# Hash attention and a gated block: three reorderings in how weight pieces are prepared

## The chip, the cores and the metric

The kernel runs on one core of one Trainium2 chip. The metric is device microseconds of that core for one whole execution; three runs of the kernel before are given, and one profiled execution with its trace.

## The reference

Attention: q, k and v are (4, 8, 768, 64). Each row of q and k is hashed with `proj` to six sign bits; a score counts only where both have the same six bits.

```python
mask = q_bucket[:, :, :, None] == k_bucket[:, :, None, :]
scores = np.where(mask, scale * np.matmul(q, k.transpose(0, 1, 3, 2)), -1e9)
attn = softmax(scores)
x = (attn @ v).transpose(0, 2, 1, 3).reshape(3072, 512)
g = x @ w_gate
out = (g / (1 + np.exp(-g)) * (x @ w_val)) @ w_out     # w_gate, w_val: 512 x 1536; w_out: 1536 x 512
```

All of it is to have fp32 accuracy.

## The kernel before

**Precision by parts.** The gated block multiplies in a faster 32-bit format and makes up for it by splitting each operand into a high part, a low part and a difference. A product is then two groups of matmuls: an `a` group (high and low, 16 matmuls) and an `n` group (differences, 8 matmuls), combined by a copy of `a` with a scale and a subtraction of `n`. All matmuls of the block are recorded on L713.

**Pieces.** The three weight matrices come as 64-bit words. They are cut into 36 pieces of 128 x 512 numbers, in the order in which they are used. `scale` (L139, L140, ScalarE) takes a piece's words apart; `widths` (L153, L155, L158, VectorE, three steps) puts the bits into fp32; `round_up` (L146, ScalarE) makes the high part; `parts` (L166, L168, VectorE, two steps) makes the other two and stores all three in DRAM (L170). `widths` ends with the load of a later piece's words (L130), three pieces on. A piece's buffer of words is one of three, its stage one of two pairs. `bring` (L251) fetches a stored piece into a ring of six buffers, on the POOL queue; in the gated block the other transfers go by SP's queue.

**Attention.** It works through 16 pairs of heads (iterations n = 0 to 15). Each scores 12 units, exponentiates them on ScalarE, adds them up on VectorE for the row sums, and multiplies by v. The row sums of pair n are made in iteration n + 1: `total` (matmuls, L590), a row copied by ScalarE (L595), a small transfer `few<-row` (L597), then `invert`: a reciprocal on VectorE (L603), a transfer to DRAM (L605) and two that spread it over partitions (L612, tile `r`). `norm` (L619) multiplies the attention output by `r` and stores it (L623). `settle()` runs the inversions that are waiting. In iteration 15 it runs twice, once at the start (pair 13) and once after the scores (pair 14); pair 15 is inverted and normalized inside the gated block, after its 6th and 14th atom. In each iteration some pieces are scaled, widened and kept (stored): 24 are scaled by the end, 22 kept.

**The gated block.** The 3072 tokens go in three blocks of 1024. Within a block there are 12 up products (U0 to U11, one per 128 columns of the hidden layer) and four down products (D0 to D3, each over three of the U); the order is U0 to U3, D0, U4 to U6, D1, U7 to U9, D2, U10, U11, D3. A U has four atoms: gate `a` with its copy (L752), gate `n` with its correction (L758) and silu (L760), value `a` with its copy (L752), value `n` with its correction (L758), the product with the gate (L762) and the hidden high part (L763). The two other hidden parts (L769, L772, the "tail") are written out after the next atom. A D has eight atoms, one per 128 tokens, here called chunks o0 to o7: nine matmuls, then in D0 a copy (L813, ScalarE) and a subtraction (L819, VectorE), in later D a multiply-add (L815) and a subtraction, both on VectorE. (D3 has four atoms more.)

**PSUM.** All products of the block take turns in four two-bank buffers, in order of creation. The `a` and the `n` of one U thus use buffers 0 to 3, and a chunk of D one buffer.

**What sets the order.** The schedule is written out by hand: every engine carries out its instructions in the order in which the code issues them. Between the atoms the block deals out preparing steps from `turns()`. One turn is, for the piece that was widened in the turn before (the old one) and the next (the new one): a rounding, a scaling, two `parts` steps, three `widths` steps; seven steps. The first turn has two old pieces and nine steps. How many steps follow each atom is a tuple: (1, 2, 2, 2) in a U, and (1, 2, 2, 1, 1, ...) in a D.

Of the kernel before, what the change touches and what calls it, by code (L numbers as in the profile page):

```python
# [19 lines left out]
def kernel(  # L20
# [68 lines left out]
    def finish(todo):  # L89
        while todo:  # L90
            todo.pop(0)()
# [31 lines left out]
    def load_words(count, queue=None):  # L123
        queue = queue or queues[0]
        for i in range(len(words), min(count, NPIECE)):
            words[i] = t = wordp.tile([P, PIECE, 2], I32, tag="words", name="words")
            to = t.rearrange("p f w -> p (f w)")
            if len(pieces[i].shape) == 3:
                to = to.rearrange("p (j c) -> p j c", j=NJ)
            queue.dma_start(to, pieces[i])  # L130

    def scale(i):
        t = words[i]
        if i // 2 not in stages:
            stages[i // 2] = stagep.tile([P, 2, 3, PIECE], FP32, tag="stage", name="stage")
        staged[i] = st = stages[i // 2][:, i % 2]
        top = t.rearrange("p f w -> p (f w)").bitcast(U16)
        top = top.rearrange("p (f w) -> p f w", w=4)[:, :, 1]
        nc.scalar.activation(st[:, 1], t[:, :, 1].bitcast(FP32), AF.Copy, scale=2.0**-112)  # L139
        nc.scalar.activation(t[:, :, 0], top, AF.Copy, scale=2.0**-13 * (1 + 2.0**-17))  # L140
        progress["scaled"] = i + 1

    def round_up(i):
        if i not in rounded:
            st = staged[i]
            nc.scalar.activation(r32(st[:, 0]), st[:, 1], AF.Copy, scale=TOWARD)  # L146
            rounded.add(i)

    def widths(i):
        t, st = words[i], staged[i]  # L150
        lo, hi = t[:, :, 0], t[:, :, 1]
        wi = st[:, 1].bitcast(I32)
        nc.vector.tensor_single_scalar(wi, wi, 3, op=ALU.logical_shift_left)  # L153
        yield True
        nc.vector.scalar_tensor_tensor(out=wi, in0=hi, scalar=-(1 << 31), in1=wi,  # L155
                                       op0=ALU.bitwise_and, op1=ALU.bitwise_or)
        yield True
        nc.vector.tensor_tensor(wi, wi, lo, op=ALU.add)  # L158
        added.add(i)
        load_words(i + 4)  # L160
        yield True

    def parts(i):
        st = staged[i]
        w = st[:, 1]
        nc.vector.tensor_tensor(r32(w), w, st[:, 0], op=ALU.subtract)  # L166
        yield True
        nc.vector.scalar_tensor_tensor(out=r32(st[:, 2]), in0=w, scalar=-STEP,  # L168
                                       in1=st[:, 0], op0=ALU.mult, op1=ALU.add)
        queues[0].dma_start(ram[i].bitcast(FP32), st)  # L170
        progress["kept"] = i + 1
        yield True

    def begin_pieces(count):
        for i in sorted(added - rounded):
            round_up(i)
        for i in range(progress["scaled"], min(progress["scaled"] + count, NPIECE)):
            load_words(i + 1)
            scale(i)

    def keep_pieces():
        for i in range(progress["kept"], progress["scaled"]):
            if i in added:
                for _ in parts(i):
                    pass

    def widen_pieces():
        for i in range(progress["kept"], progress["scaled"]):
            if i not in added:
                for _ in widths(i):  # L190
                    pass

    def turn():

        old = [i for i in sorted(added) if i >= progress["kept"]]
        new = progress["scaled"]

        def first():
            for i in old:
                round_up(i)  # L200

        def second():
            if new < NPIECE:
                load_words(new + 1)
                scale(new)

        yield first
        yield second
        for i in old:
            steps = parts(i)  # L210
            for _ in range(2):
                yield lambda: next(steps)
        if new < NPIECE:
            more = widths(new)
            for _ in range(3):
                yield lambda: next(more)
# [88 lines left out]
    def attention(scope):  # L305
# [39 lines left out]
        def load(n, names):  # L345
            if n < len(pairs):
                for name in names:
                    fetch(n, name, nc.sync)
# [187 lines left out]
        def score(u):  # L536
            if u % (2 * NCH):
                products(u)
                mark(u)
            else:  # L540
                banks_of[u] = two_banks("sc")[:, :, 0:HQ]
                product(u, bits, True, False)
                product(u, T, False, True)
                mark(u, False)
# [84 lines left out]
        def prepare_pair(count):  # L629
            for _ in range(count):  # L630
                if steps:
                    rest.extend(f for f in steps.pop(0)() or [] if f)

        def settle():
            while waiting:
                last.append(waiting.pop(0)())
# [11 lines left out]
        for n in range(len(pairs)):  # L648
            u = 2 * NCH * n
            more = n + 1 < len(pairs)  # L650
            if n == 1:
                widen_pieces()
            if n and more:
                steps = front(n + 1)
                prepare_pair(2)
            widen_pieces()
            settle()
            for i in range(2 * NCH):
                if u + i > 2:
                    score(u + i)  # L660
                if n == 0 and i == TURN:
                    prepare_pair(2)
                if i % NCH and i < 2 * NCH - 1:
                    add(u + i)
                if i == (2 if n else TURN):
                    load(n + 2, "qk")
            row = total(n - 1) if n else None
            if more:
                prepare_pair(1)
            finish(rest)  # L670
            add(u + 2 * NCH - 1)
            if row:
                row()
            finish(last)
            if not more:
                settle()
            begin_pieces(PACE[n])
            finish(splits)
            splits.extend(later)
            later.clear()  # L680
            for c in range(2 * NCH):
                attend(u + c)
            load(n + 2, "v")
            keep_pieces()
            if n >= len(pairs) - 3:
                bring()
# [14 lines left out]
    def gated_block(scope):  # L701
# [184 lines left out]
        def split_x(block, pr):  # L886
            return split(raw_x.pop((block, pr)), block, pr, 0, WB)
# [3 lines left out]
        for kind, n in order:  # L891
            b, f = divmod(n, NF if kind == "U" else NF // NQ)
            changing = b + 1 < NB
            if changing:
                if (kind, f) == ("D", NF // NQ - 2):
                    load_x(b + 1, range(NP // 2))
                elif kind == "U" and f >= NF - 2:
                    assert len(added) == NPIECE
                    splits.extend(split_x(b + 1, f - NF + 2))
                    if f == NF - 1:  # L900
                        load_x(b + 1, range(NP // 2, NP))
            if n == NB * NF // NQ - 1 and kind == "D":
                finish(tails)
            for at, atom in enumerate(atoms_of(kind, n)):
                tail = atom()
                finish(tails)
                if tail:
                    tails.append(tail)
                if changing and kind == "U" and f >= NF - 2 and at:
                    splits.pop(0)()  # L910
                if changing and kind == "D" and f == NF // NQ - 1:
                    if at == 0:
                        more = [split_x(b + 1, pr) for pr in range(NP // 2, NP)]
                        for x in more:
                            x.pop(0)()
                    if at in (7, 10):
                        for x in more:
                            x.pop(0)()
                count[0] += 1
                if left and count[0] in (6, 14):  # L920
                    left.append(left.pop(0)())
                    left[:] = [f for f in left if f]
                for _ in range(((1, 2, 2, 2) if kind == "U" else (1, 2, 2) + (1,) * 9)[at]):
                    step = next(mine, None)
                    if step:
                        step()
# [35 lines left out]
```

## Time and profile before

| What | Value |
|---|---|
| median of 3 runs | 911.25 us (910.28 to 911.82) |
| the profiled execution | 910.49 us, span in the trace 908.7 us |
| granted TensorE clock | 0.999 |
| attention, until the first matmul of the gated block | 314.80 us |
| D1, 72 matmuls | 16.32 us |
| VectorE busy, 300 to 400 us | 76.69 us |
| ScalarE busy, 300 to 400 us | 52.20 us |
| DMA, mean over the span | 192 GB/s |

A row of the page or of a timeline has a start, a duration, the engine, the line of the code and the operation, what is written and read (out<-in) with shapes, a count, and in brackets how long the engine had been idle before and what ended the idle time. PE is TensorE's matmul, PEld its weight load, DVE VectorE, ACT ScalarE, POOL GpSimd and SP SyncE (SPq: its queue). The chain of waits is followed back from the last instruction to what released each step.

### The profile page before, as it was taken

The numbers are of one execution on the slowest core, as the hardware profiler recorded it, in microseconds if no ns is written. First come the engines' busy times: TensorE is split into PE (matmuls) and PEld (weight loads), VectorE is DVE, ScalarE is ACT, GpSimd is POOL, SyncE is SP. The second block draws the span as 40 slices with busy tenths as digits, with TensorE's granted clock in tenths as the row PEclk, the third lists the DMA queues.
The fourth block names the chain that finished last, engine by engine and source line by source line (L and its number), as shares of the span: only waits on it lengthen the run. The fifth ranks groups of instructions, "written<-read, shape, count | busy, mean of one in ns | idle before, by whom it ended". The sixth has DMA issues, their size and how long they took to land.

```text
span 908.7 us, 12452 instructions
## 1 busy us (share of the span) xinstructions
PE 902.4 (99%) x4801; PEld 636.5 (70%) x4801; DVE 664.9 (73%) x783; ACT 451.5 (50%) x606; POOL 88.6 (10%) x177
## 2 busy tenths in 40 slices
PE   9999999999999999999999999999999999999998
PEld 4444444444444588788888888888888888888886
DVE  6779999998988868779786856464658754474746
ACT  7788988788887655452514233331313243413220
POOL 1001100010001210001100000101000100001000
PEclk9999999999999999999999999999999999999999
DMA  7557888878877699776756563534434642525332
GB/s 183 107 144 182 191 209 188 206 205 224 232 196 208 217 393 335 262 268 241 270 189 239 207 244 105 178 136 168 145 139 162 237 151 95 201 70 209 104 139 93
DMA packets 143706, 174.24 MB, mean 192 GB/s; under 512 B 103360, under 2 KB 113568, under 8 KB 143648
## 3 DMA queue, kind: packets, MB, share of 16 engines
q0 software_dynamic: 22240, 114.83, 35.6%
q1 hardware_dynamic: 120000, 57.43, 24.7%
q10 hardware_dynamic: 1408, 1.20, 0.5%
q8 instruction: 38, 0.62, 0.3%
q14 instruction: 20, 0.16, 0.1%
HBM read 133.17 MB, written 39.42 MB: 190 GB/s over the span
## 4 chain that ended last, share of the span: by engine, by line
PE 58%; DVE 2%; ACT 1%; issue 1%; DMA 1%; DVEq 0%; ACTq 0%; SPq 0%
PE a L713 26%; PE o L713 20%; PE n L713 13%; DMA words<-in_moe_w_out_dram 1%; DVE hid L769 0%; DVE g L758 0%; ACT v L752 0%; DVE stage L155 0%; DVE v L762 0%; DVE v L758 0%; ACT hid L763 0%; DVE o L819 0%; DVE stage L158 0%; DVE hid L772 0%; ACT o L813 0%
## 5 line engine op out<-in xcount | busy, mean ns | idle before, releaser
L713 PE MATMUL a<-xparts,ring 128*128 128x512 f32 x1152 | 273.0, 389 | 0.0
L713 PEld LDWEIGHTS a<-xparts,ring 128*128 128x128 f32 x1152 | 216.1, 188 | 45.5 <-issue 0.6
L713 PE MATMUL o<-ring,hid 128*128 128x512 f32 (+1 forms) x870 | 198.8, 388 | 1.1 <-DVE o L819 1.0
L713 PEld LDWEIGHTS o<-ring,hid 128*128 128x128 f32 x870 | 162.7, 188 | 35.6 <-DVE o L819 2.0
L533 ACT ACTIVATE A<-sc 128x768 f32<-128x768 f32 x192 | 153.9, 816 | 0.9
L523 PE MATMUL sc<-qT,kT 64*128 64x384 f32 x768 | 152.8, 483 | 0.3 <-ACT qb L436 0.2
L713 PE MATMUL n<-xparts,ring 128*128 128x512 f32 x576 | 142.3, 389 | 0.0
L554 PE MATMUL av<-A,vraw 128*64 128x386 f32 (+1 forms) x768 | 127.7, 488 | 0.0
L713 PEld LDWEIGHTS n<-xparts,ring 128*128 128x128 f32 x576 | 108.1, 188 | 22.5
L758 DVE TENSOR_TENSOR v<-v,n 128x1024 f32<-128x1024 f32 x36 | 44.0, 1222 | 99.5 <-PE n L713 97.6
L251 POOL DMA_DIRECT2D ring<-ram x108 | 57.1, 531 | 497.9 <-PE n L713 315.4
L554 PEld LDWEIGHTS av<-A,vraw 128*64 128x64 f32 x768 | 53.7, 136 | 73.3 <-issue 63.0
L752 ACT ACTIVATE g<-a 128x1024 f32<-128x1024 f32 x36 | 36.9, 1026 | 127.7 <-PE a L713 126.9
L523 PEld LDWEIGHTS sc<-qT,kT 64*128 64x128 f32 x768 | 68.3, 187 | 41.3 <-issue 35.5
L763 ACT ACTIVATE hid<-v 128x1024 fp32r<-128x1024 f32 x36 | 38.2, 1062 | 109.0 <-DVE v L762 106.4
L760 ACT ACTIVATE g<-g 128x1024 f32<-128x1024 f32 x36 | 38.2, 1062 | 88.8 <-DVE g L758 88.8
L819 DVE TENSOR_TENSOR o<-o 128x512 f32<-128x512 f32 x92 | 63.0, 686 | 19.2 <-ACT o L813 16.9
L758 DVE TENSOR_TENSOR g<-g,n 128x1024 f32<-128x1024 f32 x36 | 43.8, 1216 | 34.9 <-PE n L713 34.9
L523 PE MATMUL sc<-qb,kb 64*128 64x384 bf16 x384 | 62.8, 323 | 0.0
L572 DVE SCALAR_TENSOR_TENSOR both<-A 128x1536 f32<-128x1536 f32 x32 | 55.4, 1732 | 6.0 <-ACT A L533 4.6
L769 DVE SCALAR_TENSOR_TENSOR hid<-hid,v 128x1024 fp32r<-128x1024 f32 (+1 forms) x39 | 44.5, 1141 | 19.7 <-ACT hid L763 19.7
L576 DVE TENSOR_TENSOR both<-both,A 128x1536 f32<-128x1536 f32 x32 | 55.9, 1748 | 1.7
(80 smaller groups left out, 692.6 us busy)
## 6 DMA issues: line engine op xcount, KB each, us to landing
ring<-ram POOLq DMA_DIRECT2D x108, 768.0 KB, 5.0
ram<-stage POOLq DMA_DIRECT2D x22, 768.0 KB, 4.3
ram<-stage SPq DMA_DIRECT2D x14, 768.0 KB
vraw<-in_v_dram SPq DMA_DIRECT2D x16, 384.0 KB
out_dram<-o SPq DMA_DIRECT2D x23, 256.0 KB
kraw<-in_k_dram SPq DMA_DIRECT2D x60, 96.0 KB
qraw<-in_q_dram SPq DMA_DIRECT2D x60, 96.0 KB
r<-sums SPq DMA_DIRECT2D x30, 192.0 KB
```

What stands on the lines that cost most here:

```text
L251: nc.gpsimd.dma_start(t.bitcast(FP32), ram[at].bitcast(FP32))
L523: nc.tensor.matmul(banks_of[u][:, h], x["k", n][rows, ks], x["q", n][rows, qs], start=start, stop=stop)
L533: nc.scalar.activation(weights(u)[:, :, 0:HQ], banks_of.pop(u), AF.Exp, scale=SCALE * (1.0 if units[u][0] else OFF / 2))
L554: nc.tensor.matmul(ps[h * D : (h + 1) * D, 0:width], raws["v", n][:, h, c, :], a[:, h, 0:width], start=c == 0, stop=c == NCH - 1)
L572: nc.vector.scalar_tensor_tensor(out=t, in0=first, scalar=S * EPS / P / 2, in1=now, op0=ALU.add, op1=ALU.add)
L576: nc.vector.tensor_tensor(t, t, now, op=ALU.add)
L713: nc.tensor.matmul(ps, w, x, start=start, stop=stop)
L758: nc.vector.tensor_tensor(two(z), two(z), n_, op=ALU.subtract)
L760: nc.scalar.activation(z, z, AF.Silu)
L763: nc.scalar.activation(h, val, AF.Copy, scale=TOWARD / STEP)
L769: nc.vector.scalar_tensor_tensor(out=l_, in0=h_.bitcast(FP32), scalar=-STEP, in1=v_, op0=ALU.mult, op1=ALU.add)
L819: nc.vector.tensor_tensor(accs[c], accs[c], t[:, 1], op=ALU.subtract)
```

## The change

Three edits. In a turn, the scaling of the new piece is issued in front of the rounding of the old one. In the last iteration of attention, `settle()` is called ahead of `widen_pieces()` (in the other iterations the order stays). In down products the numbers of steps after the atoms become 0, 1, 1, 1, ... so that a D of eight atoms has seven steps, where it had ten.

```diff
@@ turn()
+        yield second
         yield first
-        yield second
         for i in old:
@@ attention
             if n and more:
                 steps = front(n + 1)
                 prepare_pair(2)
-            widen_pieces()
-            settle()
+            if more:
+                widen_pieces()
+                settle()
+            else:
+                settle()
+                widen_pieces()
@@ gated_block
-                for _ in range(((1, 2, 2, 2) if kind == "U" else (1, 2, 2) + (1,) * 9)[at]):
+                for _ in range(((1, 2, 2, 2) if kind == "U" else (0,) + (1,) * 11)[at]):
                     step = next(mine, None)
```

`first` rounds the old pieces (L146), `second` loads the new piece's words if they were not loaded and scales it (L139, L140).

## The prediction

> **What bounds the kernel now.** I read the page's busy shares first. TensorE (PE) is busy 902.4 of 908.7 us, so only what stops PE counts.
>
> ```profile
> PE 902.4 (99%) x4801; PEld 636.5 (70%) x4801; DVE 664.9 (73%) x783; ACT 451.5 (50%) x606; POOL 88.6 (10%) x177
> ```
>
> Then the waits of PE over the whole run: after the start only one real stop, in the first down product (D0, products F = 0 to 3 being U0 to U3 before it). PE's timeline places it.
>
> ```profile
> 329.48 1.98 PE L713 MATMUL n<-xparts,ring 128*128 128x512 f32 x8
> ...
> 358.50 10.36 PE L713 MATMUL o<-ring,hid 128*128 128x512 f32 x45
> 369.86 5.49 PE L713 MATMUL o<-ring,hid 128*128 128x512 f32 x21 [1.00 <-DVE o L819]
> ```
>
> Products overlap by 0.2 us in this view, so U1's gate n ends at 329.48 + 1.98 = 331.46. D0's 72 matmuls take 16.32 us where nothing stops them (D1 in the chain of waits), and D0 begins when U3's last product ends, 356.68 + 1.98 = 358.66. It would end at 374.98; in the chain U4 begins at 376.70. So D0 loses **1.7 us**. That, and about 4 us of tail that the change doesn't touch, is all there is to win.
>
> Why does D0 stop? The timelines of ScalarE (ACT) and VectorE (DVE) through U1 show a ring of waits, one round per up product:
>
> ```profile
> 336.30 1.21 DVE L758 TENSOR_TENSOR g<-g,n 128x1024 f32<-128x1024 f32 x1
> ...
> 339.16 0.69 DVE L166 TENSOR_TENSOR stage<-stage 128x512 fp32r<-128x512 f32 x1 [0.96 <-ACT stage L146]
> 340.07 1.22 DVE L758 TENSOR_TENSOR v<-v,n 128x1024 f32<-128x1024 f32 x1 [0.22 <-ACT v L752]
> 341.33 1.23 DVE L762 TENSOR_TENSOR v<-g,v 128x1024 f32<-128x1024 f32 x1
> ...
> 344.94 1.22 DVE L772 TENSOR_TENSOR hid<-hid 128x1024 fp32r<-128x1024 f32 x1
> 346.08 0.68 DVE L155 SCALAR_TENSOR_TENSOR stage<-words,stage 128x512 int32<-128x512 int32 x1
> 346.69 1.21 DVE L758 TENSOR_TENSOR g<-g,n 128x1024 f32<-128x1024 f32 x1
> ```
>
> ```profile
> 337.55 1.06 ACT L760 ACTIVATE g<-g 128x1024 f32<-128x1024 f32 x1 [3.37 <-DVE g L758]
> 338.51 0.61 ACT L146 ACTIVATE stage<-stage 128x512 fp32r<-128x512 f32 x1
> 339.03 1.01 ACT L752 ACTIVATE v<-a 128x1024 f32<-128x1024 f32 x1
> 339.94 0.65 ACT L139 ACTIVATE stage<-words 128x512 f32<-128x512 f32 x1
> 340.49 0.66 ACT L140 ACTIVATE words<-words 128x512 int32<-128x512 uint16 x1
> 342.59 1.06 ACT L763 ACTIVATE hid<-v 128x1024 fp32r<-128x1024 f32 x1 [1.44 <-DVE v L762]
> ```
>
> By differences of starts: gate correction L758 to silu L760 1.25; to rounding L146 0.96; to v's copy L752 0.52; to v's correction L758 1.04; to L762 1.26; to L763 1.26; to L769 1.09; to L772 1.26; to L155 1.14; to the next gate correction 0.61. Sum **10.39 us**, and PE's round is 2 x (3.63 + 1.81) = 10.88. So the lag of a gate correction behind its n product falls by 0.49 a round: U1 336.30 - 331.46 = 4.84, U3 357.07 - 353.22 = 3.85. The lag comes from one late row before U0's correction, the normalizing L619 of pair 14, which waits for its reciprocals:
>
> ```profile
> 324.32 1.02 DVE L619 SCALAR_TENSOR_TENSOR xT<-xT,e,r 128x768 f32<-128x768 f32 x1 [5.88 <-DMA r<-sums]
> ```
>
> D0 meets what is left of it: output chunk 5 (o5) needs the PSUM buffer of o1, whose L819 lies behind L769, L772 and L155.
>
> **The Trainium skill.** "Perfetto Trace Analysis", section Identifying the Most-Contended Engine, warns that matmul busy is no measure of PE's roofline. The trace agrees: each matmul reads 389 ns but they come every 16.32/72 = 227 ns, so I count stops, not busy time. The same page, section Optimization Strategy, says that repeated gaps can mean too few PSUM buffers; here all products share four two-bank buffers, and D0's stops are waits for one. "ScalarE: Activation LUTs", section What ACT_TABLE_LOAD costs, gives 186 ns + 0.833 ns an element and 93 ns of overlap: an estimate of 612 ns for 512, against 610 for L146, and 612 - 93 = 519 in line, against 0.52 seen. I use the trace's. "DMA: Bandwidth & Descriptors", section Issuing engines are not separate DMA queues, says transfers of all queues share 16 engines. DMA share is 0.98 to 1.08 from 315 to 320 us, when r of pair 14 travels; so its landing can't be priced from its size.
>
> **Part 1, the reciprocals of the last pair ahead of widening.** In iteration 15, L603 of pair 13 runs at 300.25 after two widenings (3.8 us) and would run at 296.5. Its few-row was issued at 291.21 with DMA idle from 291, so it is there. r then lands 3.8 earlier and the 1.1 us wait ahead of its L619 (310.90) goes. All on DVE after it comes 1.1 earlier: L603 of pair 14 at 310.7, not 311.84. SP's queue: L605 and L612 of pair 13 leave earlier, so few<-row of pair 14 leaves right behind its ACT copy (306.8, not 308.07); its landing took at most 3.8 us, so by 310.7 it is there. The two L170 stores and the loads on POOL, queued behind the same DVE work, move 1.1 earlier too and still compete with r. Value taken: r of pair 14 lands at **323.2**. Bounds: 324.3 (no gain) and 319 (uncontended, as with pair 13, L612 to L619 about 4 us). PE in attention doesn't wait for any of this: 0.
>
> **Part 2, scaling (L139, L140) ahead of rounding (L146).** A turn is 7 steps and a U takes 7, so U1 to U3 repeat: step L155 | L158, then first-of-turn | second-of-turn, L166 | L168, L153. Before, the rounding sat ahead of v's copy and L166 came just after it. Now the pair of scalings sits ahead of the copy and the rounding behind it, and L166, which stands on DVE **ahead of v's correction**, waits for that rounding. The piece of the round from silu to v's correction becomes: L760 to L139 0.97, to L140 0.55, to L752 0.56, to L146 0.92, to L166 0.65, to L758 0.61 = 4.26, where it was 0.96 + 0.52 + 1.04 = 2.52. The round grows by 1.74 to **12.13 us**, above PE's 10.88: the lag now grows by 1.25 a round. Queued behind the waiting L166 are v's correction, L762, L769 and L772; PE waits for their buffers. The DMA side: the load call in the scaling finds its words loaded, and stores follow L168; neither queue is reordered within a turn. U0 rounds two pieces; its round is 11.04 before and, with both roundings behind silu, 11.40 after.
>
> **Part 3, D takes 7 steps, not 10 (0,1,1,1,... for 1,2,2,1,...).** L155 no longer lies ahead of o1's L819 (0.6 us saved) and L146 no longer blocks o2's copy for L158 (the 0.5 us second stop). But 7 steps a D keep the turn in the same phase, so U4 to U9 all have the 12.13 round, where 10 steps used to shift it. The preparing ends in D2, not U9. Counted in code order, piece 34 is stored in U9 and brought at D2's end, 35 stored two chunks before D2's end and brought after U10's gate: no bring is late at 4 to 9 us a landing. Steps in D2 lie on DVE beside 2.04 us a chunk: 0.
>
> **The sum.** L619 323.2, U0's correction 324.14, U1's 335.54, U2's 347.67, U3's 359.80 (lag 6.6). D0's chunks start every 2.04 from 358.66.
> - o1 needs U3's g n: 359.80 + 1.26 = 361.06, wanted 360.70: stop 0.35.
> - o2 needs v's copy: 359.80 + 1.25 + 0.97 + 0.55 + 0.56 + 1.04 = 364.17, wanted 363.1: 1.05.
> - o3 needs v's correction: about 366.55, wanted 366.2: 0.35.
> - o4 needs L819 of o0: v's correction 365.3, L762 366.55, L763 367.8, L813 368.8, L819 369.4, free 0.74 later 370.1, wanted 368.6: 1.5.
> - o5 needs L819 of o1 behind L769 and L772: 369.4 + 0.6 + 1.26 + 1.14 + 0.74 = 373.1, wanted 372.2: 0.95.
>
> D0: 4.2 us. D1: U4 starts without lag, U5 1.5, U6 2.8. From U6's correction to o1's free buffer in D1 (L758 to L762 6.77, L168 and L153 1.74, L815 and L819 of o0 1.67, L769 and L772 2.40, L815 and L819 of o1 1.46) is 14.04; + 2.8 = 16.8 against 5.44 + 5 x 2.04 = 15.64: 1.2 us. D2 repeats it: 1.2. After 6.6; before, the same working gives 1.4 of the 1.7 measured. Change **+5.2 us**. The profiled execution took 910.49 (span 908.7 and 1.8 around it): 915.7. The median of the runs is 0.76 above it: **916.4**.
>
> **Rivals.**
> - r of pair 14 lands by 320, uncontended: U0's correction is then bound by PE, U3's lag is 3.75; only o4 (0.5) and o5 (0.95) stop, with D1 and D2 3.9 in all, against 1.4: +2.5, 913.7. For it: pair 13's r took 4 us. Against: DMA is full from 315 on.
> - r doesn't move: lag 7.8 at U3, 1.1 us more: 917.5.
> - Not slower: DVE's wait for the rounding stays hidden, that is the round stays under 10.88. The place is L166 in U1 to U9; the price of being wrong is 1.25 us a round. If ACT's rounding does come before v's copy, the round is about 10.4, all stops go (-1.7) and the median is 909.6. Against: each engine starts its instructions in the order written in every row I read.
>
> **Chances.** Forecast 0.54, early r 0.16, unmoved r 0.16, hidden rounding 0.10, else 0.04. 0.2% (1.8 us) is what a measurement can tell; since only 1.7 can be won, hidden rounding is "same". Faster 0.03, same 0.11, slower 0.86. The range takes in both bounds of r: 913.0 to 918.4.
>
> **What would show it.** Right: in U1 to U3, L146 after L752 of v, DVE idle ahead of L166 for ACT L146, gate corrections 12.1 us apart, stops in D0 from o1 on and one of about 1.2 in D1 and in D2, L619 near 323.2. Wrong: gate corrections 10.9 or less apart, D1 without a stop, or a stop for a ring buffer.

## The result and the profile after

The changed kernel takes 916.0 us (median of 6 runs, 915.29 to 916.3) against 910.92 for the kernel before (6 runs, 910.26 to 911.82): a ratio of 1.0056, 95% interval 1.0045 to 1.0067, so 5.1 us slower. The profiled execution took 915.62, its span is 913.8. In the changed kernel the lines behind the second edit lie four further down: L752 is now L756, L758 is L762, L762 is L766, L763 is L767, L769 and L772 are L773 and L776, L813 to L819 are L817 to L823, the matmuls are L717. Kernels without the second edit keep the old numbers.

The busy shares of the page can't tell the two kernels apart.

```profile
PE 903.6 (99%) x4801; PEld 635.7 (70%) x4801; DVE 663.5 (73%) x783; ACT 450.8 (49%) x606; POOL 88.4 (10%) x177
```

PE's timeline can. The columns are start, duration, engine, line, operation; a bracket is idle time and what ended it.

```profile
358.09 2.20 PE L717 MATMUL o<-ring,hid 128*128 128x512 f32 x9
360.49 2.34 PE L717 MATMUL o<-ring,hid 128*128 128x512 f32 x9 [0.20 <-DVE g L762]
363.61 4.75 PE L717 MATMUL o<-ring,hid 128*128 128x512 f32 x18 [0.78 <-ACT v L756]
369.54 2.35 PE L717 MATMUL o<-ring,hid 128*128 128x512 f32 x9 [1.19 <-DVE o L823]
372.54 6.41 PE L717 MATMUL o<-ring,hid 128*128 128x512 f32 x27 [0.64 <-DVE o L823]
...
411.43 10.36 PE L717 MATMUL o<-ring,hid 128*128 128x512 f32 x45
422.96 6.43 PE L717 MATMUL o<-ring,hid 128*128 128x512 f32 x27 [1.18 <-DVE o L823]
...
473.42 6.41 PE L717 MATMUL o<-ring,hid 128*128 128x512 f32 x27 [1.18 <-DVE o L823]
```

A short stop doesn't always show in PE's rows, because consecutive matmuls overlap there; the weight loads (PEld) show it. The first line is from the kernel before, the second from the changed one.

```profile
372.32 3.96 PEld L713 LDWEIGHTS o<-ring,hid 128*128 128x128 f32 x18 [0.54 <-DVE o L819]
365.98 1.93 PEld L717 LDWEIGHTS o<-ring,hid 128*128 128x128 f32 x9 [0.45 <-DVE v L762]
```

So where D0 stopped at o5 and, shortly, at o6, it now stops at each chunk from o1 to o5 (the second line is o3). D1 and D2, which ran through, each stop once, at chunk o5 (45 matmuls are five chunks). Every one of these stops ends with a step of VectorE or ScalarE that frees a PSUM buffer; none waits for a piece in the ring. U3's last product ends at 356.28 + 1.98 = 358.26, and in the chain of waits U4 begins at 378.95: D0 takes 20.7 us, where 16.32 is what it needs, so 4.4 are lost. D1 takes 17.80 us for 16.32 (from 411.43 to the start of U7 at 429.23) and loses 1.5, D2 the same. In all 7.4, where the kernel before lost 1.75.

The reason that the prediction gave, and that the experiments below test, is the order on ScalarE and VectorE. ScalarE through U1:

```profile
336.29 1.06 ACT L764 ACTIVATE g<-g 128x1024 f32<-128x1024 f32 x1 [3.37 <-DVE g L762]
337.26 0.64 ACT L139 ACTIVATE stage<-words 128x512 f32<-128x512 f32 x1
337.81 0.65 ACT L140 ACTIVATE words<-words 128x512 int32<-128x512 uint16 x1
338.35 1.01 ACT L756 ACTIVATE v<-a 128x1024 f32<-128x1024 f32 x1
339.26 0.63 ACT L146 ACTIVATE stage<-stage 128x512 fp32r<-128x512 f32 x1
```

The scalings L139 and L140 now precede v's copy (L756), and the rounding L146 comes behind it. VectorE over U0 and U1:

```profile
322.66 1.02 DVE L619 SCALAR_TENSOR_TENSOR xT<-xT,e,r 128x768 f32<-128x768 f32 x1 [5.80 <-DMA r<-sums]
...
335.04 1.21 DVE L762 TENSOR_TENSOR g<-g,n 128x1024 f32<-128x1024 f32 x1
...
339.91 0.69 DVE L166 TENSOR_TENSOR stage<-stage 128x512 fp32r<-128x512 f32 x1 [2.98 <-ACT stage L146]
340.52 1.22 DVE L762 TENSOR_TENSOR v<-v,n 128x1024 f32<-128x1024 f32 x1
...
347.13 1.21 DVE L762 TENSOR_TENSOR g<-g,n 128x1024 f32<-128x1024 f32 x1
```

The normalizing row L619 comes at 322.66, and L166 waits 2.98 us for the rounding, where it waited 0.96. v's correction (L762 at 340.52) stands behind it and starts 5.48 us after the gate's, where it started 3.77 after. From one gate correction to the next it is 12.09 us (335.04 to 347.13), not 10.39. TensorE's round is 10.88, so the lag behind it grows instead of shrinking.

### The profile page after: what moved, and what is told of

The parts are those of the page before. It is cut to its first block, busy times and chain, and to the rows that moved or that the text cites. A ratio compares the mean times of both kernels' runs of the same rounds, so it can differ in the third digit from the quotient of the medians.

```text
span 913.8 us, 12434 instructions
## 1 busy us (share of the span) xinstructions
PE 903.6 (99%) x4801; PEld 635.7 (70%) x4801; DVE 663.5 (73%) x783; ACT 450.8 (49%) x606; POOL 88.4 (10%) x177
## 4 chain that ended last, share of the span: by engine, by line
PE 51%; DVE 7%; ACT 4%; issue 2%; DVEq 0%; ACTq 0%
PE a L717 22%; PE o L717 18%; PE n L717 11%; DVE hid L773 1%; DVE v L766 1%; DVE v L762 1%; ACT v L756 1%; DVE g L762 1%; ACT hid L767 1%; DVE stage L166 1%; ACT stage L146 1%; DVE stage L155 1%; ACT stage L139 0%; DVE hid L776 0%; DVE o L823 0%
## 5 line engine op out<-in xcount | busy, mean ns | idle before, releaser
L717 PE MATMUL a<-xparts,ring 128*128 128x512 f32 x1152 | 273.0, 389 | 0.0
L717 PEld LDWEIGHTS a<-xparts,ring 128*128 128x128 f32 x1152 | 216.1, 188 | 45.5 <-issue 0.6
L717 PE MATMUL o<-ring,hid 128*128 128x512 f32 (+1 forms) x870 | 200.3, 389 | 5.2 <-DVE o L823 4.2
L717 PEld LDWEIGHTS o<-ring,hid 128*128 128x128 f32 x870 | 162.3, 188 | 41.5 <-DVE o L823 5.9
L523 PE MATMUL sc<-qT,kT 64*128 64x384 f32 x768 | 152.8, 483 | 0.2 <-ACT qb L436 0.2
L717 PE MATMUL n<-xparts,ring 128*128 128x512 f32 x576 | 142.2, 389 | 0.0
L717 PEld LDWEIGHTS n<-xparts,ring 128*128 128x128 f32 x576 | 108.1, 188 | 22.4
L762 DVE TENSOR_TENSOR v<-v,n 128x1024 f32<-128x1024 f32 x36 | 43.9, 1220 | 86.9 <-PE n L717 86.9
L756 ACT ACTIVATE g<-a 128x1024 f32<-128x1024 f32 x36 | 36.9, 1025 | 121.9 <-PE a L717 121.2
L523 PEld LDWEIGHTS sc<-qT,kT 64*128 64x128 f32 x768 | 68.2, 187 | 41.2 <-issue 35.4
L767 ACT ACTIVATE hid<-v 128x1024 fp32r<-128x1024 f32 x36 | 38.2, 1062 | 117.3 <-DVE v L766 114.2
L764 ACT ACTIVATE g<-g 128x1024 f32<-128x1024 f32 x36 | 38.2, 1061 | 92.4 <-DVE g L762 92.4
L823 DVE TENSOR_TENSOR o<-o 128x512 f32<-128x512 f32 x92 | 63.0, 687 | 19.3 <-ACT o L817 16.9
L762 DVE TENSOR_TENSOR g<-g,n 128x1024 f32<-128x1024 f32 x36 | 43.8, 1216 | 30.7 <-PE n L717 30.7
L523 PE MATMUL sc<-qb,kb 64*128 64x384 bf16 x384 | 62.8, 323 | 0.0
L773 DVE SCALAR_TENSOR_TENSOR hid<-hid,v 128x1024 fp32r<-128x1024 f32 (+1 forms) x39 | 44.5, 1141 | 19.4 <-ACT hid L767 19.4
```

What stands on the lines that cost most here:

```text
L523: nc.tensor.matmul(banks_of[u][:, h], x["k", n][rows, ks], x["q", n][rows, qs], start=start, stop=stop)
L717: nc.tensor.matmul(ps, w, x, start=start, stop=stop)
L756: nc.scalar.activation(two(z), ops[what][2], AF.Copy, scale=STEP + 1)
L762: nc.vector.tensor_tensor(two(z), two(z), n_, op=ALU.subtract)
L767: nc.scalar.activation(h, val, AF.Copy, scale=TOWARD / STEP)
L773: nc.vector.scalar_tensor_tensor(out=l_, in0=h_.bitcast(FP32), scalar=-STEP, in1=v_, op0=ALU.mult, op1=ALU.add)
```

## The experiments

Three theories were set against each other. **A**, the prediction's: a round grows because L166 stands ahead of v's correction and waits for a rounding that is now behind v's copy. **B**: what costs is that v's copy, and with it the release of its PSUM buffer, comes late behind two scalings; where L166 stands doesn't matter. **C**: the exchange is harmless, and the seven steps in a D, with preparing that lasts into D2, cost the time.

Beside the time I give two readings of each trace. *Round* is half the time from U1's gate correction to U3's. *Lost* is the time from the first matmul of U0 to the first of U10, less 157.9 us, which is what it takes in the kernel without a stop (below). These don't depend on when the attention stage begins, which varies. Each kernel is compared with runs of the kernel before that were made beside it, so the median of those differs a little from row to row (910.26 to 910.92).

| Kernel | exchange | D steps | reciprocals | U steps | round | lost | ratio to before (95%) |
|---|---|---|---|---|---|---|---|
| before | no | 10 | late | 1,2,2,2 | 10.39 | 1.75 | 1 |
| changed | yes | 7 | early | 1,2,2,2 | 12.09 | 7.4 | 1.0056 (1.0045 to 1.0067) |
| e1_swap_only | yes | 10 | late | 1,2,2,2 | 12.09 | 6.55 | 1.0048 (1.0035 to 1.006) |
| e2_no_swap | no | 7 | early | 1,2,2,2 | 10.40 | 0 | 0.9974 (0.9963 to 0.9984) |
| e3_u1132 | yes | 7 | early | 1,1,3,2 | 12.08 | 9.6 | 1.0075 (1.0061 to 1.0089) |
| e4_u1123 | yes | 7 | early | 1,1,2,3 | 10.32 | 0 | 0.9975 (0.9964 to 0.9985) |
| e5_fewer_only | no | 7 | late | 1,2,2,2 | 10.39 | 0.6 | 0.9995 (0.9987 to 1.0003) |
| e6_settle_only | no | 10 | early | 1,2,2,2 | 10.39 | 0.75 | 0.9985 (0.9978 to 0.9991) |
| e7_no_settle | yes | 7 | late | 1,2,2,2 | 12.08 | 8.1 | 1.0071 (1.0058 to 1.0084) |
| e8_no_fewer | yes | 10 | early | 1,2,2,2 | 12.09 | 4.9 | 1.0033 (1.0021 to 1.0046) |
| e9_u1213 | yes | 7 | early | 1,2,1,3 | 11.41 | 2.9 | 1.001 (1.0002 to 1.0018) |

### The exchange alone, and the change without it

```diff
# e1_swap_only, against the kernel before
+        yield second
         yield first
-        yield second
```

> The kernel before with the order of scaling and rounding exchanged, nothing else. Theory A (the subtraction L166 stands ahead of v's correction and waits for a rounding that is now behind v's copy, so a round of U1 to U3 takes 12.1 us): D0 loses about 6.5 us where the kernel before loses 1.7, D1 and D2 lose nothing because ten steps in a D shift the turn so that L166 and the rounding part; in all +4.7 us, 915.7. Theory C (the seven steps in a D, with preparing that lasts into D2, are what costs): no change, 911.

Measured: 914.98 against 910.57, +4.4 us. PE's timeline of this kernel:

```profile
361.94 2.33 PE L713 MATMUL o<-ring,hid 128*128 128x512 f32 x9 [0.98 <-DVE g L758]
365.05 4.73 PE L713 MATMUL o<-ring,hid 128*128 128x512 f32 x18 [0.78 <-ACT v L752]
370.99 2.33 PE L713 MATMUL o<-ring,hid 128*128 128x512 f32 x9 [1.20 <-DVE o L819]
374.58 6.44 PE L713 MATMUL o<-ring,hid 128*128 128x512 f32 x27 [1.26 <-DVE o L819]
...
413.50 16.48 PE L713 MATMUL o<-ring,hid 128*128 128x512 f32 x72
```

D0 stops at o1 to o5 (o3 again only in the weight loads, by 0.45), and D1 (from 413.50) runs through its 72 matmuls, both as theory A says. A short stop comes already in U3 (0.23 us idle, for v's copy). C falls as it stands: the exchange is not harmless, it costs 4.4 us with ten steps in a D.

```diff
# e2_no_swap, against the changed kernel
-        yield second
         yield first
+        yield second
```

> The changed kernel with the rounding again ahead of the scaling; reciprocals early and seven steps in a D stay. Theory A: the round is 10.4 us again, the late row before U0 comes 1.1 us earlier, no stop is left in D0, D1 and D2: -1.7 us against the kernel before, 909.3. Theory C: D1 and D2 still stop, about +3 us, 914.

Measured: 908.17 against 910.57, -2.4 us, with an interval of -0.37 to -0.16 per cent, which takes in the -1.7 expected. Its three down products in PE's timeline:

```profile
357.86 16.48 PE L717 MATMUL o<-ring,hid 128*128 128x512 f32 x72
...
406.82 16.48 PE L717 MATMUL o<-ring,hid 128*128 128x512 f32 x72
...
455.78 16.48 PE L717 MATMUL o<-ring,hid 128*128 128x512 f32 x72
```

Each is one row of 72 matmuls in 16.48 us: no stop is left. This kernel is faster than both: the other two edits together help, and the exchange costs more than they give. In the two traces the spans differ by 2.4 us as well; 1.75 of it are stops, and 0.6 come from ahead of the gated block, which begins at 314.19 here and at 314.80 in the kernel before.

### Where the exchange costs

Three kernels keep all three edits and only deal the steps of a U out differently, so that copy, rounding and L166 stand in another order.

```diff
# e3_u1132, against the changed kernel (e4_u1123: (1, 1, 2, 3); e9_u1213: (1, 2, 1, 3))
-                for _ in range(((1, 2, 2, 2) if kind == "U" else (0,) + (1,) * 11)[at]):
+                for _ in range(((1, 1, 3, 2) if kind == "U" else (0,) + (1,) * 11)[at]):
```

> The changed kernel with steps (1,1,3,2) after the atoms of a U: scaling and rounding both come behind v's copy on ScalarE, L166 stays ahead of v's correction. Theory A: the copy is early, but L166 waits as long for its rounding, the round stays near 12.1 us, D0, D1 and D2 lose about 9 us in all: 918. Theory B (what costs is that v's copy, and so its PSUM buffer, comes late behind the scaling): the copy is back at its old place, stops go, 909 to 911.

Measured: 917.57 against 910.57, +7.0 us. ScalarE, then VectorE, in U1:

```profile
336.28 1.06 ACT L764 ACTIVATE g<-g 128x1024 f32<-128x1024 f32 x1 [3.38 <-DVE g L762]
337.25 1.01 ACT L756 ACTIVATE v<-a 128x1024 f32<-128x1024 f32 x1
338.15 0.65 ACT L139 ACTIVATE stage<-words 128x512 f32<-128x512 f32 x1
338.70 0.64 ACT L140 ACTIVATE words<-words 128x512 int32<-128x512 uint16 x1
339.24 0.62 ACT L146 ACTIVATE stage<-stage 128x512 fp32r<-128x512 f32 x1
```

```profile
335.04 1.21 DVE L762 TENSOR_TENSOR g<-g,n 128x1024 f32<-128x1024 f32 x1
...
339.90 0.69 DVE L166 TENSOR_TENSOR stage<-stage 128x512 fp32r<-128x512 f32 x1 [2.97 <-ACT stage L146]
340.51 1.21 DVE L762 TENSOR_TENSOR v<-v,n 128x1024 f32<-128x1024 f32 x1
...
347.11 1.21 DVE L762 TENSOR_TENSOR g<-g,n 128x1024 f32<-128x1024 f32 x1
```

v's copy follows the silu at once, at 337.25, earlier than in the kernel before. It helps nothing: L166 still waits 2.97 us for its rounding, and the round is 12.08. B can't be the whole cause. More is lost than in the changed kernel (9.6 against 7.4), now with two stops in each of D1 and D2: in the first U after a D the copy waits for its matmuls and the scalings stand behind it, so from U4's gate correction to U5's it is 13.50 us, where the changed kernel has 12.41.

> The changed kernel with steps (1,1,2,3) after the atoms of a U: scaling and rounding behind v's copy as in the kernel with (1,1,3,2), and L166 one atom later, behind v's correction and the product with the gate. The order scaling, rounding stays exchanged. Theory A: nothing on the round waits for the rounding, a round takes under 10.9 us, no stops: -1.7 us against the kernel before, 909.3. Theory B: the same, 909 to 911. A theory in which the exchange itself costs, wherever L166 stands: 914 to 918.

Measured: 908.31 against 910.57, -2.3 us. ScalarE, then VectorE, in U1:

```profile
336.44 1.06 ACT L764 ACTIVATE g<-g 128x1024 f32<-128x1024 f32 x1 [3.77 <-DVE g L762]
337.41 1.00 ACT L756 ACTIVATE v<-a 128x1024 f32<-128x1024 f32 x1
338.31 0.66 ACT L139 ACTIVATE stage<-words 128x512 f32<-128x512 f32 x1
338.86 0.68 ACT L140 ACTIVATE words<-words 128x512 int32<-128x512 uint16 x1
339.42 0.64 ACT L146 ACTIVATE stage<-stage 128x512 fp32r<-128x512 f32 x1
```

```profile
335.19 1.22 DVE L762 TENSOR_TENSOR g<-g,n 128x1024 f32<-128x1024 f32 x1
...
338.44 1.22 DVE L762 TENSOR_TENSOR v<-v,n 128x1024 f32<-128x1024 f32 x1 [1.35 <-ACT v L756]
339.70 1.23 DVE L766 TENSOR_TENSOR v<-g,v 128x1024 f32<-128x1024 f32 x1
340.85 0.68 DVE L166 TENSOR_TENSOR stage<-stage 128x512 fp32r<-128x512 f32 x1
...
345.50 1.22 DVE L762 TENSOR_TENSOR g<-g,n 128x1024 f32<-128x1024 f32 x1
```

ScalarE has the same order as in e3_u1132: copy, scalings, rounding. Only L166 has moved, behind v's correction and the product with the gate, and starts at 340.85 without a wait. v's correction starts at 338.44, 3.25 us after the gate's; the round is 10.32, and nothing is lost. So the exchanged order costs nothing where it stands behind the copy and L166 stands behind v's correction; between this kernel and e3_u1132, L166's place makes the whole difference.

> The changed kernel with steps (1,2,1,3) after the atoms of a U: scaling ahead of v's copy and rounding behind it, as in the changed kernel, but L166 one atom later, behind v's correction and the product with the gate. It prices the late copy alone. Theory A: of the 1.74 us by which a round grew, 0.59 are the copy's (L139 and L140 for L146), 1.15 the wait of L166 with its own time; with L166 away (it and two more steps then stand ahead of the tail, some 0.4 us) the round is about 11.3 to 11.4, a little above TensorE's 10.88, and 2.5 to 3 us are lost, mostly in D0: +1 us against the kernel before, 911.5. Theory B (all of it is the copy's lateness): as the changed kernel, 916.0.

Measured: 911.09 against 910.3, +0.8 us, ratio 1.001 (1.0002 to 1.0018). ScalarE, then VectorE, in U1:

```profile
336.08 1.06 ACT L764 ACTIVATE g<-g 128x1024 f32<-128x1024 f32 x1 [3.86 <-DVE g L762]
...
338.15 1.01 ACT L756 ACTIVATE v<-a 128x1024 f32<-128x1024 f32 x1
339.05 0.62 ACT L146 ACTIVATE stage<-stage 128x512 fp32r<-128x512 f32 x1
```

```profile
334.84 1.21 DVE L762 TENSOR_TENSOR g<-g,n 128x1024 f32<-128x1024 f32 x1
...
339.19 1.22 DVE L762 TENSOR_TENSOR v<-v,n 128x1024 f32<-128x1024 f32 x1 [2.46 <-ACT v L756]
340.45 1.22 DVE L766 TENSOR_TENSOR v<-g,v 128x1024 f32<-128x1024 f32 x1
341.59 0.69 DVE L166 TENSOR_TENSOR stage<-stage 128x512 fp32r<-128x512 f32 x1
...
343.26 1.22 DVE L773 SCALAR_TENSOR_TENSOR hid<-hid,v 128x1024 fp32r<-128x1024 f32 x1
```

Here the copy is late behind the scalings as in the changed kernel, and L166 is out of the way. The round is 11.41 and 2.9 us are lost. It is 1.02 longer than in the kernel before, by two things. The late copy gives 0.59: from the silu to v's correction it is 3.11 us, and was 2.52. The third step that now stands ahead of the tail gives 0.46: from L766 to L773 it is 2.81 us, and was 2.35. The changed kernel has only the first of these. So of the 1.70 us by which its round grew, an estimated 0.59 are the copy's and 1.11 come with L166's wait. By the same estimate the late copy alone makes a round of 10.98, barely above TensorE's 10.88; no run has it alone. Part of what B says is true, as the smaller share. The 7.4 us lost can't be split in these shares: in the table, rounds of 10.3 to 10.4 lose at most 1.75 us, 11.41 loses 2.9, and about 12.1 loses 4.9 to 9.6.

### The other two edits, each alone and each left out

```diff
# e5_fewer_only, against the kernel before
-                for _ in range(((1, 2, 2, 2) if kind == "U" else (1, 2, 2) + (1,) * 9)[at]):
+                for _ in range(((1, 2, 2, 2) if kind == "U" else (0,) + (1,) * 11)[at]):
```

> The kernel before with seven steps in a D (0,1,1,...), nothing else. Theory A: o1's subtraction in D0 is no longer behind L155 (0.6 us) and o2's copy no longer behind a rounding that waits (0.5 us): the stop of 1.7 us falls to 0.5 to 0.7, -1.0 us, 910.1; D1 and D2 don't stop though preparing lasts into D2. Theory C: D1 and D2 stop, +2 us or more, 913.

Measured: 909.97 against 910.26; the ratio 0.9995 (0.9987 to 1.0003) includes both no change and the -1.0 expected, so the times alone decide nothing. The trace does: 0.6 us are lost where 1.75 were, at o5 alone, and D1 and D2 run through.

```diff
# e6_settle_only, against the kernel before
-            widen_pieces()
-            settle()
+            if more:
+                widen_pieces()
+                settle()
+            else:
+                settle()
+                widen_pieces()
```

> The kernel before with the reciprocals of the last iteration ahead of the widening, nothing else. Theory A: the normalizing row before U0 comes 1.1 us earlier, every lag up to D0 is 1.1 us less, the stop of 1.7 us falls to about 0.5: -1.1 us, 910.0. If the lag does not carry over one for one to D0: no change, 911.

Measured: 908.9 against 910.26, -1.4 us (0.9978 to 0.9991). Lost: 0.75 where it was 1.75. The rest of the 1.4 isn't explained by stops; in the one trace of each kernel the gated block begins 0.5 us earlier here (314.28 against 314.80).

e7_no_settle is the changed kernel without the edit of e6_settle_only.

> The changed kernel with the reciprocals of the last iteration at their old place. Theory A: the row before U0 is 1.1 us later again, and D0 loses 1.1 us more than in the changed kernel: 917.1, +6.2 us against the kernel before. If the stops in D0 don't depend on that row: 916.0.

Measured: 916.72 against 910.26, +6.5 us; 8.1 lost, 0.8 more than in the changed kernel, where 1.1 was expected.

e8_no_fewer is the changed kernel without the edit of e5_fewer_only.

> The changed kernel with ten steps in a D as before. Theory A: D0 loses 0.6 us more behind L155, D1 and D2 lose nothing because the turn is shifted there, instead of 1.5 each: 916.0 + 0.6 - 2.9 = 913.7 to 914.3, +3 us against the kernel before. Theory C: the cost goes with the seven steps: 911.

Measured: 913.16 against 910.26, +2.9 us; 4.9 lost, all in D0.

With the exchange, then, seven steps in a D are a loss of 2.5 us with early reciprocals (7.4 against 4.9) and of 1.6 with late ones (8.1 against 6.55), and without it a gain (1.75 to 0.6 with late reciprocals, 0.75 to 0 with early ones). What goes with it in the traces is the phase of the turn: in the changed kernel L166 waits 3.0 to 3.4 us for its rounding in every U from U4 to U9, and in e8_no_fewer in none of them.

## Why the prediction held

It said 916.4; measured 916.0. Step by step:

- **The reciprocals.** L619 of pair 14 was put 1.1 us earlier. The start of the attention stage shifts whole traces, so it is read from the first matmul of U0: 9.5, 9.8, 9.4 and 9.0 us behind it in the four kernels with late reciprocals, 8.2 to 8.6 in the seven with early ones; the means are 1.1 apart. The rival in which r lands by 320 didn't happen. What DMA traffic did to the landing was not tried apart.
- **The round.** 12.13 worked out, 12.09 measured; U0's 11.40 and 11.45. This is the step that carries the forecast.
- **The stops in D0.** Worked out: o1 0.35, o2 1.05, o3 and o4 1.85, o5 0.95. From the starts in PE's timeline (a chunk every 2.04 us): o1 360.49 - 360.13 = 0.36; o2 363.61 - 362.53 = 1.08; o3 and o4 369.54 - 367.69 = 1.85; o5 372.54 - 371.58 = 0.96. In the weight loads o3 and o4 come apart: 0.34 and 1.52.
- **D1 and D2.** 1.2 each worked out, 1.5 measured. The place is right (o5, behind o1's subtraction), and so is the moment at which its buffer comes free, 16.8 us after the end of U6's gate n product (404.17 + 1.98 = 406.15, to 422.96). The term is short at two other points. o5 was due at 411.43 + 5 x 2.04 = 421.63, 15.48 after that end and not 15.64, since the row of a product runs 0.16 into the next one: the stop is 1.33. And the 27 matmuls from o5 on take 6.27 us to U7's start, where at the pace of 72 in 16.32 they would take 6.12: another 0.15, left out of the working. The first matmul after the stop reads 0.50 us, the others 0.39.
- **The sum.** 6.6 against 7.4 lost after, 1.4 against 1.75 before, so +5.2 against +5.6 in the two traces. Their spans differ by 5.1 only, because the profiled execution of the kernel before started its attention later than the changed one: the first matmul of U0 is at 314.80 there, at 314.40 here. That 915.7 was worked out for the profiled execution and 915.62 came is therefore luck to the last tenth: 0.4 too little for the stops and 0.4 of an earlier start cancel. The 0.76 that was added for the median is 0.4 in the changed kernel.
- **Not foreseen.** At U0 ScalarE's first scaling waits for the store of a stage.

```profile
320.35 0.67 ACT L139 ACTIVATE stage<-words 128x512 f32<-128x512 f32 x1 [0.87 <-DMA ram<-stage]
```

It costs nothing, since the silu (L764) waits 1.98 us for VectorE anyway and starts at 324.84.

## What to carry to other kernels

When two steps of one engine are exchanged, look not only at the two but at what stands *behind their consumer* on the other engine: here an exchange of short steps on ScalarE made a VectorE step of 0.69 us hold up the one that frees the buffers. Add up the whole round through both engines and compare it with the bottleneck's: a round of 12.1 against 10.9 lets the lag grow by 1.2 us each time, and one of 10.4 works off a backlog. Of three small edits measured together, one can hide what the others gain; time each alone and each left out.

## What the runs showed of the hardware

- A stop of TensorE costs more than the idle time that its row shows: in D1 of the changed kernel PE's row shows 1.18 us idle, the weight loads 1.60, and 1.48 are lost.
- The attention stage takes the same time in all eleven traces, but doesn't start at the same time. From the first matmul that waits for the hash signs to the first of U0 is 303.35 us in the kernel before (11.45 to 314.80), in the changed one (11.05 to 314.40) and in e8_no_fewer (10.80 to 314.15); what lies ahead of it varies by 0.65 us, which is much beside the 1.4 us that the early reciprocals gain alone. Why it varies stays open.
- A transfer of 6 KB to DRAM took very different times. In the changed kernel's SP queue, for pair 13 (L605 issues the small transfer, L612 those that read it back and so wait for it):

```profile
296.32 0.33 SPq L605 DMA_DIRECT2D sums<-few  x1
297.78 1.45 SPq L612 DMA_DIRECT2D r<-sums  x2
```

L612 follows 1.46 us after L605 here, ahead of the loads of words, and 2.13 after it for pair 14 (310.73 to 312.86). In the kernel before, for pair 13, it was 300.50 to 306.92, 6.4 us: there one load of words of 512 KB was issued 1.8 us ahead of L605 and another 0.1 us behind it, and the 16 DMA engines were 84% busy or more from 300 to 306 us, where they were 67% and 33% busy in the two microseconds from 296 to 298 of the changed kernel. The other traffic is the likely reason; it was not varied alone.
- Of the two 32-bit formats in this kernel the block's is the faster: one of its matmuls of 512 columns leaves one record of 0.39 us, and an fp32 matmul of 384 columns in attention (L523) leaves two of 0.48 us.
